# A decode block with cached attention: scalars as single elements, P turned on VectorE, and q with x stationary

## The chip, the cores and the metric

The kernel runs on one core of a Trainium2 chip (trn2). The time is device time in microseconds (us) of one execution. A run's time is about 1.8 us longer than the span of its profile (668.85 against 667.1, for example), and the two are never mixed here. Where several runs are told, the median is given with the lowest and the highest.

Words that return: PE is the matmul engine and PEld its weight loads, DVE is VectorE, ACT is ScalarE, POOL is GpSimd, SP is SyncE, whose queue issues nearly all loads here. The stream is the sequence of transfers on the core's 16 DMA engines. SBUF is the on-chip memory, PSUM the matmul's accumulators.

## The reference

Four tokens of width 640 go through a block with two branches that are summed: attention with 32 heads over a cache of 4,096 keys and values, and a gated feed-forward branch in which one scalar scale and one scalar shift stand.

```python
xn = layernorm(x)                                  # x: (4, 1, 640) bf16
q = (xn @ wq) as (B=4, H=32, 1, Dh=128)            # wq: (640, 4096)
p = softmax(q . k_cache * Dh**-0.5)                # k_cache: (4, 32, 4096, 128)
o = (p . v_cache) as (B, 1, H * Dh) @ wo           # v_cache like k_cache, wo: (4096, 640)
z1, z2 = halves of gelu(xn @ w_in)                 # w_in: (640, 1728)
g = w_sp * layernorm(z2) + b_sp                    # w_sp and b_sp: one number each
out = x + o + (z1 * g) @ w_out                     # w_out: (864, 640)
```

The two caches are 268 MB of the 282 MB that the kernel must read, and every byte of them is used once.

## The kernel before

Heads go in four groups of eight. Each group has four units of K and four of V (one for each token), 8.4 MB each. All of them pass through one large SBUF tile, `kv`, cut into slots; a load into a slot can start only when the last reader of the slot's old contents is done. The parts that the change touches:

```python
# two scalars, each broadcast to 128 partitions, on POOL's software queue
sb_bf = const.tile([P, 2], BF16)
nc.gpsimd.dma_start(out=sb_bf[:, 0:1], in_=B_w_sp.rearrange("a b -> (a b)").to_broadcast((P, 1)))
nc.gpsimd.dma_start(out=sb_bf[:, 1:2], in_=B_b_sp.to_broadcast((P, 1)))
...
# q: wq stationary, 160 matmuls with four columns each
for h in range(H):
    for c in range(DC):
        nc.tensor.matmul(q_ps[:, h, :], lhsT=wq[:, c, h * Dh:(h + 1) * Dh], rhs=xnT[:, c, :], ...)
...
# softmax of one group: exp four times over, PE transposes, copies, first fill of Zb
for half in range(2):
    x = ps_t.tile([P, 16, P], BF16, tag="x", name="x")
    for q in (2 * half, 2 * half + 1):
        p_q = ppool.tile([P, 8, HP, NE, M], BF16, tag="p", name="p")
        for e in range(NE):
            nc.scalar.activation(out=p_q[:, :, :, e, :], in_=S_ps[...].to_broadcast((P, 8, HP, M)), func=ACT.Exp, ...)
        for t in range(8):
            nc.tensor.transpose(x[:, 8 * (q % 2) + t, :], p_q[:, t].rearrange("p r e m -> p (r e m)"), IdP[:])
    for hp in range(HP):
        nc.vector.tensor_copy(out=xd[r0:r0 + 32, :, 16 * half:16 * half + 16], in_=x[r0:r0 + 32, :, r0:r0 + 32]...)
    z_fill(g, 0, (slice(16 * half, 16 * half + 16),))
z_fill(g, 1)
```

`Zb` holds the probabilities in the form in which 64 matmuls (called the O matmuls below) take them as weights against one unit of V. The first V load after a softmax overwrites a slot that these O matmuls still read, so the chain from scores to O matmuls decides when that load is issued.

## Time and profile before

| | before |
|---|---|
| time, median of 3 runs | 668.84 us (668.02 to 668.85) |
| profiled span | 665.9 us |
| bytes read from memory | 282.25 MB |
| mean rate over the span | 424 GB/s |
| busiest engine | DVE, 54% |
| TensorE | 46% |

A busy share says how much of the span an engine worked. The row that matters here is DMA in the 40 slices, shown in the prediction: it stands at 9 from the second slice to the last but one, so the kernel is bound by its stream. The groups of instructions that the change replaces are small beside that. From the page's groups (line, engine, operation, output from input, count, then busy us and mean ns, then idle time before):

```profile
L414 DVE COPY xd<-x 32x512 bf16<-32x512 bf16 x32 | 22.0, 687 | 20.7 <-PE x L410 20.0
L410 PE MATMUL x<-IdP,p 128*128 128x128 bf16 x128 | 16.5, 309 | 25.2 <-ACT p L406 12.9
...
L258 PE MATMUL misc<-xnT,kv 128*128 128x4 bf16 x160 | 4.4, 166 | 7.8 <-DMA kv<-in_A_wq_dram 7.8
```

The last row is q: PE waits 7.8 us for wq and is then busy for 4.4. The two rows above it are the turning of P, together with the copies behind it. They are there four times, once for each group of heads.

### The profile page before, as it was taken

To read this page: it belongs to the slowest core of one execution; us is meant where nothing else is said; L and a number is where in the kernel's file an instruction comes from. 1 tells how busy PE (TensorE), PEld (TensorE's weight loads), DVE (VectorE), ACT (ScalarE), POOL (GpSimd) and SP (SyncE) were. 2 spreads that over 40 slices of the span, in tenths; PEclk is the share of its full clock that TensorE was granted. 3 is DMA by queue.
4 is the path that set the end of the run, shared out by engine and by line. 5 is a ranking of instruction groups with operands and counts; after the bars stand their busy time and mean duration, and the time that the engine had idled before them with its cause. 6 is when DMAs were issued, how large, how long until landed. Compare 5 with 4: busy or idle time off the path is not lost.

```text
span 665.9 us, 6036 instructions
## 1 busy us (share of the span) xinstructions
PE 306.5 (46%) x2585; PEld 126.8 (19%) x2585; DVE 358.0 (54%) x318; ACT 93.3 (14%) x233; POOL 8.0 (1%) x27
## 2 busy tenths in 40 slices
PE   0656656526063546535425065551605336543355
PEld 0512211302011122211102022230201112122122
DVE  5179998446190749428356186743709165852002
ACT  1200000730200000450200000082020000046200
POOL 1000000000000000000000000000000000000000
PEclk9996787569578596676959587765867868677776
DMA  8999999999999999999999999999999999999996
GB/s 327 434 422 433 436 425 448 437 427 437 426 437 438 437 403 449 429 438 441 426 429 438 425 420 428 449 426 438 433 442 441 426 433 408 439 434 434 434 408 243
DMA packets 7874, 282.64 MB, mean 424 GB/s; under 512 B 948, under 2 KB 1320, under 8 KB 2088
## 3 DMA queue, kind: packets, MB, share of 16 engines
q1 hardware_dynamic: 7768, 282.25, 98.5%
q8 instruction: 20, 0.33, 0.2%
q14 instruction: 6, 0.05, 0.0%
q10 hardware_dynamic: 16, 0.01, 0.0%
q0 software_dynamic: 64, 0.00, 0.0%
HBM read 282.25 MB, written 0.01 MB: 424 GB/s over the span
## 4 chain that ended last, share of the span: by engine, by line
DMA 76%; DVE 10%; issue 10%; PE 2%; ACT 1%; DVEq 0%; SPq 0%; ACTq 0%
DMA kv<-in_A_k_cache_dram 66%; DVE kT L348 9%; DMA kv<-in_A_v_cache_dram 4%; DMA kv<-in_A_wo_dram 3%; DMA kv<-in_A_wq_dram 3%; PE misc L258 1%; ACT Zb L392 1%; ACT p L406 1%; DVE xd L414 1%; PE O L437 0%; PE proj L475 0%; PE x L410 0%; DVE om L457 0%; DVE m L366 0%; PE S L359 0%
## 5 line engine op out<-in xcount | busy, mean ns | idle before, releaser
L348 DVE STREAM_TRANSPOSE kT<-kv 128x2048 f32<-128x2048 f32 x128 | 283.4, 2277 | 134.2 <-DMA kv<-in_A_k_cache_dram 134.2
L359 PE MATMUL S<-kT,QZ 128*32 128x512 bf16 x1024 | 189.9, 505 | 237.5 <-DVE kT L348 237.5
L359 PEld LDWEIGHTS <-QZ 128*32 128x32 bf16 x1024 | 60.8, 112 | 359.9 <-issue 340.3
L437 PE MATMUL O<-kv,Zb 128*32 128x512 bf16 x1024 | 70.8, 431 | 34.4 <-DMA kv<-in_A_v_cache_dram 23.9
L392 ACT ACTIVATE Zb<-xd,MkE 32x256 bf16<-32x256 bf16 (+1 forms) x160 | 65.3, 454 | 108.3 <-PE O L437 99.1
L406 ACT ACTIVATE p<-S,negmax 128x512 bf16<-128x512 f32 x32 | 21.6, 694 | 398.2 <-DVE negmax L380 398.2
L444 DVE TENSOR_SCALAR R<-O,Mk 128x128 f32<-128x128 f32 x16 | 5.6, 351 | 106.2 <-PE O L437 106.2
L437 PEld LDWEIGHTS <-Zb 128*32 128x32 bf16 x1024 | 34.1, 106 | 69.2 <-issue 44.2
L414 DVE COPY xd<-x 32x512 bf16<-32x512 bf16 x32 | 22.0, 687 | 20.7 <-PE x L410 20.0
L410 PE MATMUL x<-IdP,p 128*128 128x128 bf16 x128 | 16.5, 309 | 25.2 <-ACT p L406 12.9
L410 PEld LDWEIGHTS <-p 128*128 128x128 bf16 x128 | 12.3, 140 | 30.2 <-ACT p L406 16.9
L454 PE MATMUL misc<-R,SelR 128*32 128x128 f32 x32 | 6.7, 293 | 24.0 <-DVE R L446 24.0
L446 DVE SCALAR_TENSOR_TENSOR R<-O,Mk,R 128x128 f32<-128x128 f32 x48 | 16.8, 351 | 1.7
L335 POOL COPY QZ<-q 32x32 bf16<-32x32 bf16 x16 | 5.1, 319 | 412.1 <-PE S L359 400.9
L475 PE MATMUL proj<-kv,oT 128*4 128x320 bf16 x64 | 8.4, 426 | 1.2 <-DMA kv<-in_A_wo_dram 1.0
L454 PEld LDWEIGHTS misc<-R,SelR 128*32 128x32 f32 x32 | 2.4, 112 | 31.4 <-DVE R L446 31.1
L366 DVE TENSOR_REDUCE m<-S 128x2 f32<-128x1024 f32 x4 | 4.9, 1225 | 6.0 <-PE S L359 6.0
L258 PE MATMUL misc<-xnT,kv 128*128 128x4 bf16 x160 | 4.4, 166 | 7.8 <-DMA kv<-in_A_wq_dram 7.8
L406 ACT ACTIVATION_READ_ACCUMULATOR p<-S,negmax 128x1 f32 x32 | 6.8, 212 | 0.0
L371 PE MATMUL misc<-dg,ones_f 128*128 128x256 f32 x8 | 3.0, 466 | 7.5 <-DVE dg L368 7.5
L457 DVE SCALAR_TENSOR_TENSOR om<-misc,rinv,MkH 32x1024 bf16<-32x1024 f32 x4 | 5.1, 1272 | 2.6 <-PE misc L454 2.6
L261 DVE CAST q_bf<-misc 128x128 bf16<-128x128 f32 x1 | 0.3, 292 | 11.3 <-PE misc L258 11.3
(92 smaller groups left out, 62.2 us busy)
## 6 DMA issues: line engine op xcount, KB each, us to landing
kv<-in_A_k_cache_dram SPq DMA_DIRECT2D x14, 4096.0 KB, 33.0
kv<-in_A_wq_dram SPq DMA_DIRECT2D x1, 5120.0 KB
kv<-in_A_v_cache_dram SPq DMA_DIRECT2D x1, 4096.0 KB, 38.4
kv<-in_A_wo_dram SPq DMA_DIRECT2D x2, 1280.0 KB, 28.7
kv<-in_B_w_in_dram SPq DMA_DIRECT2D x1, 2160.0 KB, 22.0
kv<-in_A_v_cache_dram SPq DMA_DIRECT2D x1, 2048.0 KB, 32.0
kv<-in_A_wo_dram SPq DMA_DIRECT2D x3, 640.0 KB, 20.7
kv<-in_A_v_cache_dram SPq DMA_DIRECT2D x1, 1536.0 KB
```

The source lines that it names most:

```text
L258: nc.tensor.matmul(q_ps[:, h, :], lhsT=wq[:, c, h * Dh:(h + 1) * Dh], rhs=xnT[:, c, :], start=(c == 0), stop=(c == DC - 1))
L348: nc.vector.transpose(kT[:].rearrange("p (t r) -> p t r", r=32), kw)
L359: nc.tensor.matmul(S_ps[32 * q:32 * q + 32, e], lhsT=QZ[:, b, 2 * kh + w, e, w0:w0 + 32], rhs=kb[:, i, :, e, :, w], start=(b == 0 and k < ...
L392: nc.scalar.activation(out=dst, in_=src, func=ACT.Copy, scale=MkE[r0:r0 + 32, e:e + 1])
L406: nc.scalar.activation(out=p_q[:, :, :, e, :], in_=S_ps[:, e, 8 * q:8 * q + 8, None, :].to_broadcast((P, 8, HP, M)), func=ACT.Exp, bias=ne ...
L410: nc.tensor.transpose(x[:, 8 * (q % 2) + t, :], p_q[:, t].rearrange("p r e m -> p (r e m)"), IdP[:])
L414: nc.vector.tensor_copy(out=xd[r0:r0 + 32, :, 16 * half:16 * half + 16], in_=x[r0:r0 + 32, :, r0:r0 + 32].rearrange("p t r -> p r t"))
L437: nc.tensor.matmul(O_ps[32 * q:32 * q + 32, :, :], lhsT=Zb[b % 2][:, w].rearrange("p h c -> p (h c)"), rhs=vv[:, w * 4 * Dh:(w + 1) * 4 * ...
L444: nc.vector.tensor_scalar(out=R, in0=O_ps[:, 0, :], scalar1=Mk4[:, 0:1], scalar2=None, op0=ALU.mult)
L446: nc.vector.scalar_tensor_tensor(out=R, in0=O_ps[:, c, :], scalar=Mk4[:, c:c + 1], in1=R, op0=ALU.mult, op1=ALU.add)
L454: nc.tensor.matmul(oh[:], lhsT=SelR[:, b].rearrange("p h b -> p (h b)"), rhs=state["R"][:, b, :], start=(b == 0), stop=(b == B - 1))
L475: nc.tensor.matmul(proj[32 * hf:32 * hf + B, 0:NO2], lhsT=oT[:, c, :], rhs=wo_t[g][:, c, hf * NO2:(hf + 1) * NO2], start=False, stop=(g == ...
```

## The change

Three things are done at once. The scalars are loaded as two single elements and spread to 128 partitions by a matmul with a row of ones. P is turned by one vector transpose of 32x32 blocks, followed by copies from quadrant to quadrant, half on DVE and half on ACT; exp is then computed once instead of four times. And q is computed with x as the weights and wq moving, which needs 40 matmuls for 160, and copies after them.

```diff
-    sb_bf = const.tile([P, 2], BF16)
-    nc.gpsimd.dma_start(out=sb_bf[:, 0:1], in_=B_w_sp.rearrange("a b -> (a b)").to_broadcast((P, 1)))
-    nc.gpsimd.dma_start(out=sb_bf[:, 1:2], in_=B_b_sp.to_broadcast((P, 1)))
+    sb_bf = const.tile([1, 2], BF16)                      # behind w_out on the SP queue
+    nc.sync.dma_start(out=sb_bf[:, 0:1], in_=B_w_sp)
+    nc.sync.dma_start(out=sb_bf[:, 1:2], in_=B_b_sp[None, :])
     ... cut ...
+            for j in range(NG):
+                nc.tensor.matmul(q4_ps[32 * j:32 * j + 32, hf * 512:hf * 512 + 512], lhsT=xnT[:, c, :],
+                                 rhs=wq[:, c, n0:n0 + 512], start=(c == 0), stop=(c == DC - 1))
     ... cut: eight copies of q4, half on DVE and half on ACT, then 32 small matmuls that select q3 ...
-    nc.gpsimd.tensor_copy(out=sb_f[:], in_=sb_bf[:])
+    nc.tensor.matmul(sb_ps[:], lhsT=one_bf[:], rhs=sb_bf[:], start=True, stop=True)
+    nc.vector.tensor_copy(out=sb_f[:], in_=sb_ps[:])
     ... cut: in softmax, the loops shown above are replaced by ...
+        for e in range(NE):
+            nc.scalar.activation(out=p_bf[:, :, e, :], in_=S_ps[:, e], func=ACT.Exp, ..., accum_out=rowsum[:, e:e + 1])
+        nc.vector.transpose(pT[:].rearrange("p t h x -> p (t h x)"), p_bf[:].rearrange("p t e m -> p (t e m)"))
+        for hp in range(HP):
+            for q in range(4):
+                op = nc.vector.tensor_copy if q < 2 else nc.scalar.copy
+                op(out=xd[32 * hp:32 * hp + 32, :, q, :], in_=pT[32 * q:32 * q + 32, :, hp, :].rearrange("p t x -> p x t"))
+        z_fill(g, 0)
         z_fill(g, 1)
```

More of the change, by code (lines that the diff above doesn't have):

```diff
@@ L68 @@
     ppool = ctx.enter_context(tc.tile_pool(name="ppool", bufs=3))
-    ps_t = ctx.enter_context(tc.tile_pool(name="ps_t", bufs=1, space=bass.MemoryType.PSUM))
     ps_s = ctx.enter_context(tc.tile_pool(name="ps_s", bufs=1, space=bass.MemoryType.PSUM))
     ps_o = ctx.enter_context(tc.tile_pool(name="ps_o", bufs=2, space=bass.MemoryType.PSUM))
-    ps_m = ctx.enter_context(tc.tile_pool(name="ps_m", bufs=1, space=bass.MemoryType.PSUM))
+    ps_m = ctx.enter_context(tc.tile_pool(name="ps_m", bufs=2, space=bass.MemoryType.PSUM))
     ps_j = ctx.enter_context(tc.tile_pool(name="ps_j", bufs=1, space=bass.MemoryType.PSUM))
@@ L102 @@
     nc.vector.memset(x_res[:], 0.0)
-    sb_bf = const.tile([P, 2], BF16)
-    nc.gpsimd.dma_start(out=sb_bf[:, 0:1], in_=B_w_sp.rearrange("a b -> (a b)").to_broadcast((P, 1)))
-    nc.gpsimd.dma_start(out=sb_bf[:, 1:2], in_=B_b_sp.to_broadcast((P, 1)))
-    sb_f = const.tile([P, 2], F32)
     n_in = DC * F2
@@ L191 @@
         nc.tensor.transpose(xT_ps[:, c, :], xn_v[:, c, :], ident_bf[:B, :B])
-    xnT = const.tile([P, DC, B], BF16)
-    nc.vector.tensor_copy(out=xnT[:], in_=xT_ps[:])
+    xnT = const.tile([P, DC, 32], BF16)
+    nc.vector.memset(xnT[:], 0.0)
+    nc.vector.tensor_copy(out=xnT[:, :, 0:B], in_=xT_ps[:])
     QL = 40
@@ L224 @@
     nc.vector.tensor_reduce(out=MkE[:], in_=I32[:].rearrange("p (e m) -> p e m", e=NE), axis=AX.X, op=ALU.add)
-    IdP = const.tile([P, P], BF16)
-    nc.vector.tensor_copy(out=IdP[:].rearrange("p (x q) -> p q x", q=4), in_=ident_bf[:].rearrange("p (q x) -> p q x", q=4))
     IdF = const.tile([P, P], F32)
@@ L232 @@
     nc.vector.tensor_reduce(out=MkH[:], in_=ident_f[:G, :G].rearrange("p (h b) -> p h b", b=B), axis=AX.X, op=ALU.add)
-    nc.vector.tensor_scalar(out=MkH[:], in0=MkH[:], scalar1=float(HP), scalar2=None, op0=ALU.mult)
     B32f = const.tile([G, B], F32)
@@ L237 @@
     nc.vector.tensor_copy(out=B32[:], in_=B32f[:])
-    Pm = const.tile([P, 4, HP, 32], BF16)
-    for hp in range(HP):
-        nc.vector.tensor_copy(out=Pm[:, :, hp, :].rearrange("p (a w) j -> p a w j", w=2),
-                              in_=ident_bf[:].rearrange("p (a j w) -> p a w j", a=2, w=2))
     NW = T // 4
@@ L252 @@
     proj = ps_j.tile([64, 512], F32)
-    q_ps = misc_ps([P, H, B], F32)
-    for h in range(H):
+    q4_ps = ps_s.tile([P, HG * Dh], F32, tag="S", name="q4")
+    for hf in range(2):
         for c in range(DC):
-            nc.tensor.matmul(q_ps[:, h, :], lhsT=wq[:, c, h * Dh:(h + 1) * Dh], rhs=xnT[:, c, :],
-                             start=(c == 0), stop=(c == DC - 1))
-    q_bf = const.tile([P, H * B], BF16)
-    nc.vector.tensor_copy(out=q_bf[:], in_=q_ps[:].rearrange("p h b -> p (h b)"))
-    q3_ps = misc_ps([P, 4, H * B], F32)
-    for kw in range(4):
-        nc.tensor.matmul(q3_ps[:, kw, :], lhsT=Pm[:, kw, :, :].rearrange("p a j -> p (a j)"), rhs=q_bf[:],
-                         start=True, stop=True)
-    q3 = const.tile([P, 4, H * B], BF16)
+            for j in range(NG):
+                n0 = j * HG * Dh + hf * 512
+                nc.tensor.matmul(q4_ps[32 * j:32 * j + 32, hf * 512:hf * 512 + 512], lhsT=xnT[:, c, :],
+                                 rhs=wq[:, c, n0:n0 + 512], start=(c == 0), stop=(c == DC - 1))
+    q4 = at_slot(0, HG * Dh * HP, n_q + 8 * D).rearrange("p (h k r j) -> p h k r j", h=HG, k=4, r=HP)
+    q4_in = q4_ps[:].rearrange("p (h a j w) -> p h a w j", h=HG, a=2, w=2)
+    for r in range(HP):
+        op = nc.vector.tensor_copy if r < 2 else nc.scalar.copy
+        for a in range(2):
+            op(out=q4[:, :, 2 * a:2 * a + 2, r, :], in_=q4_in[:, :, a])
+    SelJ = const.tile([P, NG, B], BF16)
+    nc.vector.tensor_copy(out=SelJ[:], in_=ident_bf[:].rearrange("p (j r) -> p j r", j=NG)[:, :, 0:B])
+    q3_ps = misc_ps([P, 4, HG, NG * B], F32)
+    for h in range(HG):
+        for kw in range(4):
+            nc.tensor.matmul(q3_ps[:, kw, h, :], lhsT=q4[:, h, kw].rearrange("p r j -> p (r j)"),
+                             rhs=SelJ[:].rearrange("p j b -> p (j b)"), start=True, stop=True)
+    q3 = const.tile([P, 4, HG, NG * B], BF16)
     nc.vector.tensor_copy(out=q3[:], in_=q3_ps[:])
@@ L280 @@
                 nc.tensor.matmul(zT_ps[:n, part, fc, :], lhsT=w,
-                                 rhs=xnT[:, c, :], start=(c == 0), stop=(c == DC - 1))
+                                 rhs=xnT[:, c, 0:B], start=(c == 0), stop=(c == DC - 1))
     zT = const.tile([P, 2, FC, B], F32)
@@ L287 @@
     nc.scalar.activation(out=zT[:FL, :, FC - 1, :], in_=zT_ps[:FL, :, FC - 1, :], func=ACT.Gelu_apprx_tanh)
-    nc.gpsimd.tensor_copy(out=sb_f[:], in_=sb_bf[:])
+    one_bf = const.tile([1, P], BF16)
+    nc.vector.memset(one_bf[:], 1.0)
+    sb_ps = misc_ps([P, 2], F32)
+    nc.tensor.matmul(sb_ps[:], lhsT=one_bf[:], rhs=sb_bf[:], start=True, stop=True)
+    sb_f = const.tile([P, 2], F32)
+    nc.vector.tensor_copy(out=sb_f[:], in_=sb_ps[:])
     z1 = zT[:, 0, :, :]
@@ L333, in fill_qz @@
             r0 = 32 * hp
-            c0 = (g * HG + NE * hp) * B
             nc.gpsimd.tensor_copy(out=QZ[r0:r0 + 32, :, :, :, 8 + 8 * hp],
-                                  in_=q3[r0:r0 + 32, :, c0:c0 + NE * B].rearrange("p a (e b) -> p b a e", b=B))
+                                  in_=q3[r0:r0 + 32, :, NE * hp:NE * hp + NE, g * B:g * B + B].rearrange("p a e b -> p b a e"))
     state = {}
@@ L381, in softmax_max, with z_fill @@
         return negmax
-    def z_fill(g, b, halves=(slice(0, TC),)):
+    def z_fill(g, b):
         xd = state[("xd", g)]
-        for hs in halves:
-            n0, n1 = hs.start // 4, hs.stop // 4
-            for hp in range(HP):
-                r0 = 32 * hp
-                src = xd[r0:r0 + 32, 8 * b:8 * b + 8, hs].rearrange("p x (y c) -> p x y c", c=4)
-                for e in range(NE):
-                    dst = Zb[b % 2][r0:r0 + 32, :, NE * hp + e, :].rearrange("p (x y) c -> p x y c", x=8)[:, :, n0:n1, :]
-                    nc.scalar.activation(out=dst, in_=src, func=ACT.Copy, scale=MkE[r0:r0 + 32, e:e + 1])
+        for hp in range(HP):
+            r0 = 32 * hp
+            src = xd[r0:r0 + 32, C2 * b:C2 * b + C2].rearrange("p x q (y c) -> p (x q y) c", c=4)
+            for e in range(NE):
+                nc.scalar.activation(out=Zb[b % 2][r0:r0 + 32, :, NE * hp + e, :], in_=src, func=ACT.Copy,
+                                     scale=MkE[r0:r0 + 32, e:e + 1])
     def softmax(g):
@@ L396, in softmax @@
         S_ps = state.pop(("S", g))
-        xd = small.tile([P, 32, TC], BF16, tag="xd", name="xd", bufs=1)
-        state[("xd", g)] = xd
-        rs = small.tile([P, NE, 4], F32, tag="rs")
-        for half in range(2):
-            x = ps_t.tile([P, 16, P], BF16, tag="x", name="x")
-            for q in (2 * half, 2 * half + 1):
-                p_q = ppool.tile([P, 8, HP, NE, M], BF16, tag="p", name="p")
-                for e in range(NE):
-                    nc.scalar.activation(out=p_q[:, :, :, e, :],
-                                         in_=S_ps[:, e, 8 * q:8 * q + 8, None, :].to_broadcast((P, 8, HP, M)),
-                                         func=ACT.Exp, bias=negmax[:, e:e + 1], scale=scale, accum_out=rs[:, e, q:q + 1])
-                for t in range(8):
-                    nc.tensor.transpose(x[:, 8 * (q % 2) + t, :], p_q[:, t].rearrange("p r e m -> p (r e m)"), IdP[:])
-            for hp in range(HP):
-                r0 = 32 * hp
-                nc.vector.tensor_copy(out=xd[r0:r0 + 32, :, 16 * half:16 * half + 16],
-                                      in_=x[r0:r0 + 32, :, r0:r0 + 32].rearrange("p t r -> p r t"))
-            z_fill(g, 0, (slice(16 * half, 16 * half + 16),))
+        p_bf = ppool.tile([P, TC, NE, M], BF16, tag="p", name="p")
+        rowsum = small.tile([P, NE], F32, tag="rowsum")
+        for e in range(NE):
+            nc.scalar.activation(out=p_bf[:, :, e, :], in_=S_ps[:, e], func=ACT.Exp, bias=negmax[:, e:e + 1], scale=scale,
+                                 accum_out=rowsum[:, e:e + 1])
+        pT = ppool.tile([P, TC, HP, B * C2], BF16, tag="p", name="pT")
+        nc.vector.transpose(pT[:].rearrange("p t h x -> p (t h x)"), p_bf[:].rearrange("p t e m -> p (t e m)"))
+        xd = small.tile([P, B * C2, 4, TC], BF16, tag="xd", name="xd", bufs=1)
+        state[("xd", g)] = xd
+        for hp in range(HP):
+            for q in range(4):
+                op = nc.vector.tensor_copy if q < 2 else nc.scalar.copy
+                op(out=xd[32 * hp:32 * hp + 32, :, q, :], in_=pT[32 * q:32 * q + 32, :, hp, :].rearrange("p t x -> p x t"))
+        z_fill(g, 0)
         z_fill(g, 1)
-        rowsum = small.tile([P, NE], F32, tag="rowsum")
-        nc.vector.tensor_reduce(out=rowsum[:], in_=rs[:], axis=AX.X, op=ALU.add)
         cs = misc_ps([G, 1], F32)
@@ L431, in emit_V @@
         vv = unit(("v", v))
-        order = list(range(NW))
-        if b == 0:
-            order.sort(key=lambda w: w % 8 // 4)
-        for n, w in enumerate(order):
-            q = n % 4
+        for w in range(NW):
+            q = w % 4
             nc.tensor.matmul(O_ps[32 * q:32 * q + 32, :, :], lhsT=Zb[b % 2][:, w].rearrange("p h c -> p (h c)"),
-                             rhs=vv[:, w * 4 * Dh:(w + 1) * 4 * Dh], start=(n < 4), stop=(n >= NW - 4))
+                             rhs=vv[:, w * 4 * Dh:(w + 1) * 4 * Dh], start=(w < 4), stop=(w >= NW - 4))
         if b == 0:
```

## The prediction

> **What bounds the kernel now.** I read the page's 40 slices first, then the chain that ended last, the stretches of the first and last microseconds, and the DMA queue's own timeline. The slices:
>
> ```profile
> DVE  5179998446190749428356186743709165852002
> ...
> DMA  8999999999999999999999999999999999999996
> GB/s 327 434 422 433 436 425 448 437 427 437 426 437 438 437 403 449 429 438 441 426 429 438 425 420 428 449 426 438 433 442 441 426 433 408 439 434 434 434 408 243
> ```
>
> From the second slice to the last but one the DMA row never leaves 9, while every engine has idle slices. The page reads 282.25 MB from HBM; the stretch from 8.75 to 650 us shows a DMA share of 1.00 at 432 GB/s. So 282.25 / 0.432 = 653 us of the 665.9 us are transfer, and only three things can move the end: bytes (the change leaves them alone, apart from a few hundred), holes in the stream, and what runs before its start and after its end. The chain agrees:
>
> ```profile
> DMA 76%; DVE 10%; issue 10%; PE 2%; ACT 1%; DVEq 0%; SPq 0%; ACTq 0%
> ```
>
> A warning on that row: its DVE pieces (10%) are a transpose of K that frees a slot, followed by a transfer that lands 30 us later. Between the two the transfer mostly stands in the queue behind others, so these pieces are no cost either. What matters is how long a transfer queues. The K loads take 33.0 us from issue to landing and the V loads 34.9, while an 8.4 MB unit by itself takes 8.39 / 0.432 = 19.4 us: some 14 us of slack. The tightest case is the V load issued at 607.04 us, which lands at 636.14: 29.1 - 19.4 = 9.7 us.
>
> The stream has one visible hole. Stretches of the first microseconds (columns: stretch, length, busy time of five engines, clock, DMA share, GB/s; a packet counts where it starts, so a share may exceed 1):
>
> ```profile
> 4.00:5.00 1.00, 0.00 (x0) 0.00 (x0) 1.00 (x2) 0.00 (x0) 0.00 (x0) 1.00 1.15 492
> 5.00:6.00 1.00, 0.00 (x0) 0.00 (x0) 0.98 (x5) 0.00 (x0) 0.00 (x0) 1.00 0.11 41
> 6.00:7.00 1.00, 0.00 (x0) 0.00 (x0) 0.95 (x2) 0.00 (x0) 0.00 (x0) 1.00 0.21 82
> 7.00:8.00 1.00, 0.00 (x0) 0.00 (x0) 0.99 (x4) 0.29 (x1) 0.00 (x0) 1.00 1.27 533
> ```
>
> The wq rows are packets of 40 KB that take about 1.5 us each. Fifteen of the 16 engines start their second packet at 4.3 to 4.8 us and would be free again at 5.9 to 6.3; yet nearly all start the third only at 6.9 to 8.1. In the packet records of this trace each of these late starts comes 12 ns after a 16-byte packet of the software queue, which carries nothing but the two broadcast scalars:
>
> ```profile
> q0 software_dynamic: 64, 0.00, 0.0%
> ```
>
> Means: free at 6.0, next start at 7.75, so about 1.75 us lost per engine. Later packets of 40 KB follow each other without a gap.
>
> **What the Trainium skill says.** "DMA: Bandwidth & Descriptors", section "Queues, rings and completion order": each DMA engine goes round-robin between the queue rows that have work, a packet at a time. The trace agrees as far as it shows 16-byte packets between the 40 KB ones; that an engine stands still until the software queue's packet can run is my reading, not the page's. Same page, "Why a DMA increments its semaphore by 16 and not by 1": a one-element transfer on the hardware queue uses one engine alone. No run shows it yet; it means that the new scalar loads can delay one engine only, by a packet or two. "VectorE: DVE Perf Modes", "The three transpose paths": the vector transpose turns 32x32 blocks and cannot span banks, hence the copies between quadrants. Its 2,048-element fp32 transpose takes 2,277 ns here, 1.11 ns per column element; I take the same for 1,024 elements of bf16.
>
> **The change part by part.**
>
> *Scalars.* Two software-queue broadcasts (128 elements each) go; two one-element loads join the SP queue behind w_out, and a 1x128 matmul spreads them. They should land with w_out at some 24 us; they are needed at about 31 us, where the scale and shift now stands. Effect on the stream: the hole closes, -1.75 us; against it some 0.1 us on one engine. Since the last bytes come from the slowest of 16 engines I count -1.6.
>
> *q with x stationary.* Before: 160 weight loads and matmuls, 18.09 to 22.54 = 4.45 us, then 0.30 (copy), 0.6 (4 matmuls), 0.7 (copy): q3 at 24.2. After: 40 matmuls of 512 columns over four column groups. The O matmuls are of this form: 64 in 3.64 us, 0.057 each; so 40 x 0.057 + 0.3 = 2.6 us. Then four copies of 128x512 from PSUM on DVE (0.69 us, like the q cast) beside four on ACT (0.69, like exp): 2.8. Then 32 matmuls with full weight loads at 0.05 = 1.6, and the cast 0.7. Sum 7.7 against 6.1: q3 some 1.6 us later, or level with before if wq lands 1.7 us earlier. K1's first half, which needs wq's slot, was issued at 22.9 us and is only due to run when wq, w_in, w_out and K0 (16.9 MB) are through, about 43 us; its second half, which now also waits for q4 in that slot, is due ten us later. The first K transpose waits for its DMA until 36.2 us; the vector work before it ended at 31.6. All of this is hidden.
>
> *Softmax.* Its last instance, in order of the chain:
>
> ```profile
> 591.63 2.80 ACT p L406 x8
> ...
> 594.47 1.05 PE x L410 x8
> ...
> 595.61 0.68 DVE xd L414
> ...
> 598.49 0.68 ACT Zb L392 x2
> ...
> 604.35 0.69 ACT Zb L392 x2
> ...
> 605.08 1.94 PE O L437 x32
> 607.04 29.11 DMA kv<-in_A_v_cache_dram
> ```
>
> Before: from 591.54 (negmax) to 607.04, 15.5 us, with eight exps, 32 PE transposes, eight copies of 0.69 us and, on ACT, sixteen fills of 0.34 us on the way to the first V unit. After: two exps (2 x 0.90 with their accumulator reads = 1.8), one transpose of 1,024 elements (1.15), then eight copies of 32x256 on each of DVE and ACT (ACT at 0.41 between starts, as a fill of that size: 3.3; DVE less), eight fills of 0.46 (3.7), then 64 matmuls (3.6). Sum 13.5: the V load is issued about 2 us sooner. The slack it had was 9.7 us, so its landing does not move. Per group DVE saves about 2 us and PE 4 us, and ACT loses six exps but gains eight copies; none of them is on the path.
>
> *Tail.* The instructions after the last V piece are the same ones in the same order (I compared the PE streams: only semaphore numbers differ, and one wait goes). From 655.9 us the old tail took 10 us, and the new one should too.
>
> *Instruction fetches.* PE's program shrinks from 5,081 rows to 4,643. Before, 20 fetches of 16 KB ran on the same DMA engines, one holding an engine for about 1 us, and they are part of why the engines finish spread out:
>
> ```profile
> 657.00:658.00 1.00, 0.50 (x6) 0.24 (x7) 0.93 (x3) 0.00 (x0) 0.00 (x0) 0.50 0.76 303
> 658.00:659.00 1.00, 1.00 (x8) 0.60 (x5) 0.10 (x1) 0.00 (x0) 0.00 (x0) 0.50 0.55 221
> 659.00:660.00 1.00, 1.00 (x9) 0.35 (x7) 0.81 (x1) 0.00 (x0) 0.00 (x0) 0.50 0.52 202
> 660.00:661.00 1.00, 0.74 (x10) 0.48 (x8) 0.46 (x1) 0.00 (x0) 0.00 (x0) 0.55 0.31 119
> ```
>
> One or two fetches fewer are worth 0 to 1 us, depending on whether the slowest engine is spared; I count -0.2.
>
> Sum: 668.84 - 1.6 - 0.2 = 667.0 us.
>
> **Rivals.** (1) The hole belongs to the start of the hardware queue (its first descriptors), and the software packets merely wait beside it. For it: other things start then too, and the second software transfer, near 10.5 us, opens no hole. Against it: sixteen late starts, each right behind a software packet. Then the time stays at 668.5 to 669. (2) A wait takes the place of the one removed: the longer q chain or the copies on ACT hold back K's slots or the first V unit. For it: ACT does fill, copy and exp in one line. Against it: 20 us of slack at the start and 9.7 at the end. Copies of twice the estimated time would still be hidden; a gap of 5 us would need an error of 15, and would give 674. (3) The compute saved shortens the run as such, 2 us in each of four softmaxes: 660. The full DMA row speaks against it. (4) The engines' spread shifts with the fetches and the slowest gets one more: up to +1 us on either outcome.
>
> **Range and chances.** I give the closed hole two chances in three (666 to 668), the unchanged one a little under one in three (668 to 669.5). The spread of the engines adds a microsecond either way, so 664.8 to 669.3. Two per cent is 13 us: more than all time outside the stream, so faster is next to impossible, and slower needs a stall that the slack speaks against.
>
> **What would show it.** Right: the software queue gone from the list of queues; a DMA share near 1 in the stretch from 5 to 8 us; wq's first reader on PE at about 16.4 us instead of 18.09; the middle at 432 GB/s; the last V load still landing one unit's time after the one before it. Wrong: an empty stretch at 5 to 7 us as before (step 1); a hole in the DMA row near 115 to 140 us or 590 to 610 us, or the first K transpose waiting for PE or ACT instead of its DMA (the slack); a tail longer than 10 us from the last V matmul.

## The result, and the profile after

| | before | after |
|---|---|---|
| time, median of 6 runs | 668.88 us (668.02 to 669.06) | 666.77 us (665.57 to 666.91) |
| profiled span | 665.9 us | 665.0 us |
| instructions | 6,036 | 5,565 |
| q's first matmul on PE starts at | 18.09 us | 16.16 us |
| last V unit multiplied: first DVE step on it starts at | 656.59 us | 654.73 us |

The ratio is 0.9965, with a 95% interval of 0.9952 to 0.9978. Ratios here are the mean time of one kernel's fast runs over that of the other's of the same rounds, so they are not quite the ratio of the medians quoted. The change takes 2.1 us off, 0.3%.

The runs of both kernels fall in two clusters about 1 us apart: before mostly near 668.9 and some near 668.0, after near 666.8 and 665.6. The two profiles fell in different ones (the profiled run of before took 667.67 us, below all six timed ones, that of after 666.74), so their spans (665.9 and 665.0) understate the gain. The tail below shows it. The last row of the table is free of that, since it comes before the tail's last matmuls, and it moved by 1.86 us.

From the page of the kernel after, the rows of DMA and of the rate, its queues and its chain:

```profile
DMA  9999999999999999999999999999999999999995
GB/s 372 424 440 425 426 441 444 438 431 439 434 418 439 434 413 455 434 427 438 419 434 439 434 418 421 452 442 434 427 426 431 438 439 412 464 418 423 429 415 219
...
q1 hardware_dynamic: 7772, 282.25, 98.6%
q8 instruction: 18, 0.29, 0.2%
...
DMA 74%; DVE 10%; issue 10%; PE 3%; ACT 2%; DVEq 0%; SPq 0%; ACTq 0%
```

The first slice rose from 327 to 372 GB/s and the software queue is gone from the list. The rest of the row is as full as it was. The first microseconds of the kernel after (columns: stretch, length, busy time with count of PE, PEld, DVE, ACT and POOL, clock, DMA share, GB/s):

```profile
5.00:6.00 1.00, 0.00 (x0) 0.00 (x0) 1.00 (x5) 0.00 (x0) 0.00 (x0) 1.00 1.51 655
6.00:7.00 1.00, 0.00 (x0) 0.00 (x0) 0.97 (x4) 0.00 (x0) 0.00 (x0) 1.00 0.19 82
7.00:8.00 1.00, 0.00 (x0) 0.00 (x0) 0.99 (x3) 0.21 (x1) 0.00 (x0) 1.00 1.32 573
```

The 0.19 in the middle is no hole. A packet counts where it starts, and the packets are 40 KB each; over the three microseconds the mean is 437 GB/s, where before it was 219 (41, 82 and 533).

The new groups, from the page's groups:

```profile
L417 ACT COPY xd<-pT 32x256 bf16<-32x256 bf16 x32 | 19.6, 613 | 5.7 <-DVE pT L410 5.2
...
L417 DVE COPY xd<-pT 32x256 bf16<-32x256 bf16 x32 | 11.7, 364 | 0.6
...
L410 DVE STREAM_TRANSPOSE pT<-p 128x1024 bf16<-128x1024 bf16 x4 | 5.0, 1245 | 6.3 <-ACT p L406 6.3
```

And the last softmax on the timeline (start, duration, instructions, idle time before and what ended it):

```profile
592.01 5.02 ACT L417 COPY xd<-pT 32x256 bf16<-32x256 bf16 x8 [1.31 <-DVE pT L410]
...
597.06 7.39 ACT L397 ACTIVATE Zb<-xd,MkE 32x256 bf16<-32x256 bf16 x16
600.79 6.08 PE L434 MATMUL O<-kv,Zb 128*32 128x512 bf16 x64 [9.78 <-ACT Zb L397]
606.92 10.87 SPq L148 DMA_DIRECT2D kv<-in_A_v_cache_dram  x5
```

Negmax was ready at 589.16, so this chain took 17.8 us to the issue of the V load; before it took 15.5. The end of the tail, first on the timeline of before and then on that of after:

```profile
661.45 1.25 PE L475 MATMUL proj<-kv,oT 128*4 128x320 bf16 x16 [0.28 <-DVE oT L468]
```

```profile
659.58 2.30 PE L472 MATMUL proj<-kv,oT 128*4 128x320 bf16 x16 [0.28 <-DVE oT L465]
```

The same sixteen matmuls start 1.87 us sooner and take 1.05 us longer, at a granted clock of 0.50 in this profile and 1.00 in that of before. That is the difference between the spans' 0.9 us and the 1.9 us of the table.

### The profile page after: what moved, and what is told of

It is laid out like the page before. It is cut to its first block, busy times and chain, and to the rows that moved or that the text cites. A ratio compares the mean times of both kernels' runs of the same rounds, so it can differ in the third digit from the quotient of the medians.

```text
span 665.0 us, 5565 instructions
## 1 busy us (share of the span) xinstructions
PE 294.0 (44%) x2366; PEld 111.6 (17%) x2366; DVE 353.5 (53%) x319; ACT 91.3 (14%) x189; POOL 6.2 (1%) x24
## 3 DMA queue, kind: packets, MB, share of 16 engines
q1 hardware_dynamic: 7772, 282.25, 98.6%
## 4 chain that ended last, share of the span: by engine, by line
DMA 74%; DVE 10%; issue 10%; PE 3%; ACT 2%; DVEq 0%; SPq 0%; ACTq 0%
DMA kv<-in_A_k_cache_dram 65%; DVE kT L356 9%; DMA kv<-in_A_v_cache_dram 4%; DMA kv<-in_A_wo_dram 3%; DMA kv<-in_A_wq_dram 2%; PE O L434 1%; PE q L252 1%; ACT xd L417 1%; PE proj L472 1%; ACT Zb L397 0%; DVE kv L260 0%; PE S L367 0%; ACT kv L260 0%; ACT p L406 0%; DVE om L454 0%
## 5 line engine op out<-in xcount | busy, mean ns | idle before, releaser
L367 PE MATMUL S<-kT,QZ 128*32 128x512 bf16 x1024 | 185.7, 495 | 232.2 <-DVE kT L356 232.2
L434 PE MATMUL O<-kv,Zb 128*32 128x512 bf16 x1024 | 75.2, 457 | 66.2 <-ACT Zb L397 39.1
L397 ACT ACTIVATE Zb<-xd,MkE 32x256 bf16<-32x256 bf16 x128 | 57.7, 497 | 106.5 <-PE O L434 105.1
L406 ACT ACTIVATE p<-S,negmax 128x512 bf16<-128x512 f32 x8 | 5.4, 683 | 395.1 <-DVE negmax L388 395.1
L417 ACT COPY xd<-pT 32x256 bf16<-32x256 bf16 x32 | 19.6, 613 | 5.7 <-DVE pT L410 5.2
L417 DVE COPY xd<-pT 32x256 bf16<-32x256 bf16 x32 | 11.7, 364 | 0.6
L410 DVE STREAM_TRANSPOSE pT<-p 128x1024 bf16<-128x1024 bf16 x4 | 5.0, 1245 | 6.3 <-ACT p L406 6.3
L260 DVE CAST kv<-q 128x512 bf16<-128x512 f32 x4 | 2.5, 682 | 9.4 <-PE q L252 9.4
L252 PE MATMUL q<-kv,xnT 128*32 128x512 bf16 x40 | 4.5, 629 | 5.1 <-DMA kv<-in_A_wq_dram 5.1
L422 PE MATMUL misc<-rowsum,SelPe 128*32 128x1 f32 x16 | 2.1, 200 | 9.0 <-ACT p L406 9.0
```

The source lines that it names most:

```text
L252: nc.tensor.matmul(q4_ps[32 * j:32 * j + 32, hf * 512:hf * 512 + 512], lhsT=xnT[:, c, :], rhs=wq[:, c, n0:n0 + 512], start=(c == 0), stop= ...
L367: nc.tensor.matmul(S_ps[32 * q:32 * q + 32, e], lhsT=QZ[:, b, 2 * kh + w, e, w0:w0 + 32], rhs=kb[:, i, :, e, :, w], start=(b == 0 and k < ...
L397: nc.scalar.activation(out=Zb[b % 2][r0:r0 + 32, :, NE * hp + e, :], in_=src, func=ACT.Copy, scale=MkE[r0:r0 + 32, e:e + 1])
L406: nc.scalar.activation(out=p_bf[:, :, e, :], in_=S_ps[:, e], func=ACT.Exp, bias=negmax[:, e:e + 1], scale=scale, accum_out=rowsum[:, e:e + 1])
L417: op(out=xd[32 * hp:32 * hp + 32, :, q, :], in_=pT[32 * q:32 * q + 32, :, hp, :].rearrange("p t x -> p x t"))
L434: nc.tensor.matmul(O_ps[32 * q:32 * q + 32, :, :], lhsT=Zb[b % 2][:, w].rearrange("p h c -> p (h c)"), rhs=vv[:, w * 4 * Dh:(w + 1) * 4 * ...
```

## The experiments

**How to read them.** Since the clock of the tail blurs a single span, and the medians mix the two clusters, I read each run at three places: its median, the start of the DVE step that follows the last V unit (called R), and the mean rate over a fixed stretch in which its hole lies. In the runs on scalars R measures what the stream lost before it. Both R and the rate come from one profile of each kernel, and a profiled run can lie apart from the others of its kernel (before's was 0.35 us below its fastest timed run, e6's 0.5 above its next slowest), so differences of half a microsecond in them are not read as effects. All runs gave correct results.

| run | scalars | median (lowest to highest) | ratio to before | R |
|---|---|---|---|---|
| before | two broadcasts, software queue, at the start | 668.88 (668.02 to 669.06) | 1 | 656.59 |
| after | single elements, SP queue | 666.77 (665.57 to 666.91) | 0.9965 | 654.73 |
| e1_scalars_only | before + single elements, SP queue | 666.90 (666.23 to 666.95) | 0.9971 | 654.68 |
| e2_no_scalars | after + the old broadcasts | 668.98 (668.01 to 669.03) | 1.0002 | 656.90 |
| e3_hw_broadcast | before + two broadcasts on the SP queue | 668.14 (668.10 to 668.82) | 0.9995 | 656.13 |
| e4_late_sw | before + software broadcasts later | 668.93 (668.57 to 669.12) | 1.0002 | 656.49 |
| e5_sw_single | before + single elements, software queue | 667.18 (666.26 to 667.24) | 0.9968 | 655.01 |
| e6_distinct | e1 + two loads of 128 elements, rows apart | 666.00 (665.94 to 667.40) | 0.9960 | 655.46 |
| e7_double | e3 with four broadcasts | 670.15 (669.54 to 671.37) | 1.0017 | 659.26 |
| e12_adjacent | e1 + two loads of 128 adjacent elements | 667.88 (667.02 to 668.28) | 0.9983 | 656.39 |

### Which part of the change

The theory: the gain is the scalars alone, and the other two parts are hidden behind the stream. The rival: the shorter compute is worth something too.

**e1_scalars_only**: the kernel before with the scalars' part of the change and nothing else.

```diff
-    nc.gpsimd.dma_start(out=sb_bf[:, 0:1], in_=B_w_sp...to_broadcast((P, 1)))   # and one for b_sp
+    nc.sync.dma_start(out=sb_bf[:, 0:1], in_=B_w_sp)                            # and one for b_sp
-    nc.gpsimd.tensor_copy(out=sb_f[:], in_=sb_bf[:])
+    nc.tensor.matmul(sb_ps[:], lhsT=one_bf[:], rhs=sb_bf[:], start=True, stop=True)
+    nc.vector.tensor_copy(out=sb_f[:], in_=sb_ps[:])
```

> The kernel before with the scalar part of the change alone. Theory (the software-queue broadcasts hold every DMA engine at the start; nothing else of the change counts): the whole gain, 666.6 to 667.0 us against 668.9 (-2.0), the first q matmul at 16.2 us instead of 18.09, a DMA share near 1.5 in the stretch from 5 to 6 us. Rival A (the shorter PE program, two instruction fetches fewer, makes the gain): 668.9, since PE's program is not shorter here. Rival B (the compute saved in q and softmax makes it): 668.9.

It measured 666.90 us, ratio 0.9971 (0.9959 to 0.9984), and R at 654.68 against 654.73 of the full change. This is the whole gain. It has 20 instruction fetches, as before, so the two that the full change saves are not needed for it.

**e2_no_scalars**: the full change, with the old broadcasts put back.

```diff
-    nc.sync.dma_start(out=sb_bf[:, 0:1], in_=B_w_sp)                            # and one for b_sp
+    nc.gpsimd.dma_start(out=sb_bf[:, 0:1], in_=B_w_sp...to_broadcast((P, 1)))   # and one for b_sp
```

> The changed kernel with the two software-queue broadcasts put back. Theory: no gain, 668.5 to 669.1 us, hole from 5 to 7 us back, first q matmul at 18.1 us. Rival A: it keeps up to 1 us of gain (667.9). Rival B: it keeps the gain (666.8).

It measured 668.98 us, ratio 1.0002 (0.9989 to 1.0014). Its first microseconds:

```profile
5.00:6.00 1.00, 0.00 (x0) 0.00 (x0) 1.00 (x5) 0.00 (x0) 0.00 (x0) 1.00 0.09 41
6.00:7.00 1.00, 0.00 (x0) 0.00 (x0) 0.93 (x3) 0.00 (x0) 0.00 (x0) 1.00 0.32 123
```

The hole is back and with it the time. q, softmax and the 18 fetches together are worth nothing that these rounds can tell from zero.

### What makes the hole

The prediction put it down to the software queue: an engine stands still until that queue's packet can run. Rivals: the broadcast itself does it, on any queue; or it is the start of the stream, beside which the packets merely wait.

**e4_late_sw**: the kernel before, with the same two software broadcasts held back until the layernorm's result; they are issued at 11.92 and 12.59 us.

```diff
+    nc.gpsimd.tensor_copy(out=sb_bf[:], in_=xnT[:, 0, 0:2])    # makes the loads wait
     nc.gpsimd.dma_start(out=sb_bf[:, 0:1], in_=B_w_sp...to_broadcast((P, 1)))
```

> The kernel before with the software-queue broadcasts issued only after the normalised x exists, at about 10.5 us. If the first software packet on an engine always holds it: the hole moves to about 13 to 17 us and the time stays at 668.5 to 669.1. If the hole needs the coincidence with the start of the stream: first q matmul at 16.2 us, no hole later, 666.6 to 667.2 us.

The time stayed (668.93 us), but the hole left its place. Over 5 to 8 us the rate is now 437 GB/s, as in the kernel after, and it stands here instead, with the same mean of 219 GB/s over 15 to 18 us:

```profile
15.00:16.00 1.00, 0.00 (x0) 0.00 (x0) 0.00 (x0) 0.00 (x0) 0.00 (x0) 1.00 0.85 328
16.00:17.00 1.00, 0.77 (x29) 0.77 (x29) 0.00 (x0) 0.00 (x0) 0.00 (x0) 1.00 0.13 35
```

The hole travels with the loads of the scalars. The rival of the stream's start is out.

**e3_hw_broadcast**: the same two broadcasts, on the SP queue behind w_out, and nothing on the software queue.

```diff
-    nc.gpsimd.dma_start(out=sb_bf[:, 0:1], in_=B_w_sp...to_broadcast((P, 1)))
+    nc.sync.dma_start(out=sb_bf[:, 0:1], in_=B_w_sp...to_broadcast((P, 1)))     # behind w_out; b_sp likewise
```

> The kernel before with the same two 128-element broadcasts issued from the SP queue behind w_out. If the software queue is what holds the engines: the gain is kept, 666.6 to 667.2 us, first q matmul at 16.2 us. If it is the 256 two-byte elements, whatever queue carries them: no gain, or the hole moves to where they run, behind w_out, 668.5 to 669.

There is no hole at the start, and q begins at 16.00 us; but a hole opens where these loads stand in the queue:

```profile
22.00:23.00 1.00, 0.81 (x18) 0.81 (x18) 0.14 (x1) 0.00 (x0) 0.72 (x3) 1.00 0.78 232
23.00:24.00 1.00, 1.00 (x23) 1.00 (x21) 0.00 (x0) 0.00 (x0) 0.60 (x2) 1.00 0.28 96
```

The time is 668.14 us, ratio 0.9995 (0.9981 to 1.0009). The software queue is not needed for the loss.

**e5_sw_single**: the reverse, the kernel before with single elements on the software queue at the start.

```diff
-    nc.gpsimd.dma_start(out=sb_bf[:, 0:1], in_=B_w_sp...to_broadcast((P, 1)))
+    nc.gpsimd.dma_start(out=sb_bf[:, 0:1], in_=B_w_sp)          # tile [1, 2]; b_sp likewise; matmul as in e1
```

> The kernel before with the scalars as single elements (and the spreading matmul), but still issued on the software queue at the start. If the count of two-byte elements makes the hole: nearly the whole gain, 666.7 to 667.3 us, first q matmul at 16.2 us. If the mere use of the software queue at the start makes it: 668.5 to 669 us, first q matmul near 18 us.

667.18 us, ratio 0.9968 (0.9954 to 0.9982), and 437 GB/s over 5 to 8 us, although the queue still has its 64 packets. So the use of the queue does not make the hole; what costs is the broadcast, on either queue. One observation stays unexplained: on the software queue the whole hole comes with the first broadcast. The packets of the second, near 10.5 us in before, open none: over 8 to 11 us that kernel moves 437 GB/s, as the kernel after does.

**e7_double**: e3 with four broadcasts in place of two.

```diff
+    nc.sync.dma_start(out=dummy[:, 0:1], in_=B_b_sp.to_broadcast((P, 1)))       # and the same into dummy[:, 1:2]
```

> The kernel of the third run (both broadcasts on the SP queue behind w_out) with two more unused broadcasts right behind them, four in all. If each broadcast costs its elements: the hole doubles and the time grows by another 1.2 us, to 669.2 to 669.7. If the hole is paid once for the kind of transfer: 668.1 to 668.4.

670.15 us, and R 3.1 us later than in e3. The hole is now five microseconds long:

```profile
22.00:23.00 1.00, 0.88 (x20) 0.88 (x20) 0.07 (x1) 0.00 (x0) 0.79 (x3) 1.00 0.63 184
23.00:24.00 1.00, 1.00 (x22) 1.00 (x21) 0.00 (x0) 0.00 (x0) 0.55 (x2) 1.00 0.10 23
24.00:25.00 1.00, 1.00 (x25) 1.00 (x24) 0.00 (x0) 0.00 (x0) 0.00 (x0) 1.00 0.20 66
25.00:26.00 1.00, 0.82 (x14) 0.73 (x13) 0.00 (x0) 0.14 (x2) 0.18 (x1) 1.00 0.34 131
26.00:27.00 1.00, 0.42 (x2) 0.45 (x2) 0.27 (x2) 0.98 (x3) 0.00 (x0) 1.00 0.42 164
```

### What it is about a broadcast

A broadcast to 128 partitions is 128 elements of two bytes, all from one address. Is it the small elements, or the address?

**e6_distinct**: e1, and two more loads of 128 elements that nobody uses, from rows 1,280 bytes apart.

```diff
+    nc.sync.dma_start(out=dummy[:, 0:1], in_=B_w_out[0:P, 0:1])
+    nc.sync.dma_start(out=dummy[:, 1:2], in_=B_w_out[P:2 * P, 0:1])
```

> The kernel with the scalar part alone, plus two unused loads of 128 two-byte elements from 256 different HBM addresses, on the SP queue behind w_out, where the broadcasts of the third run stood. If small elements as such hold the engines: about 668.1 us as there, with a hole near 22 to 24 us. If it is that all 128 reads of a broadcast go to one address: 666.7 to 667.2 us and no hole of that size.

**e12_adjacent**: the same with the 128 elements side by side, 256 bytes in all.

```diff
-    nc.sync.dma_start(out=dummy[:, 0:1], in_=B_w_out[0:P, 0:1])
+    nc.sync.dma_start(out=dummy[:, 0:1], in_=B_w_out[0:1, 0:P].rearrange("a n -> n a"))   # and row 1 likewise
```

> As the run with distinct rows (the scalars as single elements, and two unused loads of 128 two-byte elements on the SP queue behind them), except that each unused load now takes its 128 elements from adjacent addresses, 256 bytes in a row, instead of from 128 rows 1,280 bytes apart. Theory A, the engines are held because all reads of a broadcast go to one and the same address: no hole at 22 to 25 us, median 666.0 to 667.0. Theory B, it is enough that the reads fall into one small region of memory: a hole of some 2 us at 22 to 25 us as with the two broadcasts on the SP queue, median 668.1 to 669. A hole of about half the size with 667 to 668 would mean that both count.

e6 measured 666.00 us and e12 667.88. I had first read e6 to mean that only reads of one and the same address hold the engines. e12 does not bear that out: its addresses all differ, and it has a hole.

```profile
22.00:23.00 1.00, 0.98 (x22) 0.98 (x22) 0.00 (x0) 0.00 (x0) 0.85 (x3) 1.00 0.62 194
23.00:24.00 1.00, 1.00 (x22) 1.00 (x21) 0.00 (x0) 0.00 (x0) 0.48 (x2) 1.00 0.48 162
```

The mean rate from 20 to 30 us sizes them all on one scale. e1 has 445 GB/s there. A run with the rate r lost 10 us times (445 - r) / 445:

| run | extra loads behind w_out | GB/s over 20 to 30 us | lost, us | R later than e1, us |
|---|---|---|---|---|
| e1_scalars_only | none | 445 | 0 | 0 |
| e6_distinct | 2 x 128 elements, 1,280 bytes apart | 415 | 0.7 | 0.8 |
| e3_hw_broadcast | 2 x 128 elements, one address | 374 | 1.6 | 1.5 |
| e12_adjacent | 2 x 128 elements, adjacent | 370 | 1.7 | 1.7 |
| e7_double | 4 x 128 elements, one address | 274 | 3.8 | 4.6 |

(In e3 and e7 these loads stand in place of e1's single elements, in e6 and e12 beside them.) The size depends on the stretch that is taken: over 18 to 32 us the five rates are 422, 422, 387, 386 and 311 GB/s, which gives 0, 0, 1.2, 1.2 and 3.7 us. So 256 elements of two bytes cost 1.2 to 1.7 us when their addresses are close together, whether equal or adjacent, and between nothing and 0.7 us when they are far apart. That e6 lost anything is not shown: its profiled run, at 667.40 us, was the slowest of its five, and cluster by cluster its times (666.90 and 667.40; 665.94 to 666.00) lie about e1's (666.71 to 666.95; 666.23). Theory A of e12, one and the same address, falls, since e12 has a hole. Theory B, one small stretch of memory, fits the stream, where e12 loses as much as e3. The median does not settle it: 667.88 us lies in the band, 667 to 668, that the expectation had given to both counting, so whether equal addresses add something is open. e1 and e3 ran on one chip, e5, e6 and e7 on a second, e12 on a third, which the last column does not correct for; e5, with single elements, has R at 655.01. What in the memory or the engines makes close addresses slow is not shown by any of these runs.

### How much slack the softmax had

Theory: the copies on ACT are off the path, with microseconds to spare. Rival: the slack is so small that a little more puts a hole behind each softmax.

**e8_act_once**: the kernel after with all sixteen copies of a softmax on ACT, none on DVE. **e9_act_twice**: the same, and each copy made twice.

```diff
-            for q in range(4):
-                op = nc.vector.tensor_copy if q < 2 else nc.scalar.copy
+            for q in range(4):               # e9: for q in [0, 1, 2, 3] * 2
+                op = nc.scalar.copy
```

> The changed kernel with all sixteen copies between quadrants of each softmax on ACT (none on DVE): the softmax chain grows by 8 x 0.63 = 5.0 us. In the changed kernel's trace the last such V load is issued at 606.9 us and its data starts to move at about 634.5 - 19.4 = 615.1. Theory (the softmax hides behind the queue): no change, 666.7 to 667.1 us. If the softmax were on the path: 671 us for the last group alone.

> As the run before, but every one of the sixteen copies is made twice: the softmax chain grows by 24 x 0.63 = 15.1 us. That is more than the 8.2 us of slack of the last group and about the 15 us of the others. Theory: a hole of some 7 to 9 us near 616 to 624 us and up to 1 us in each of the three others: 674 to 678 us. If something else than the queue absorbs it: less than 670.

Both are misses. e8 took 668.64 us (667.72 to 669.99, 4 runs; ratio to before 1.0001, 0.9987 to 1.0014), 1.9 us more than the kernel after; e9 took 706.21 us (703.49 to 708.62; ratio 1.056, 1.0534 to 1.0586), 39 us more. Stretches of e8 around its last softmax, and of e9 around its first:

```profile
610.00:615.00 5.00, 3.62 (x44) 1.26 (x36) 1.22 (x4) 2.46 (x6) 0.00 (x0) 0.75 0.98 368
615.00:620.00 5.00, 4.19 (x68) 2.05 (x68) 0.81 (x3) 2.97 (x8) 0.00 (x0) 1.00 0.58 236
```

```profile
136.00:140.00 4.00, 0.00 (x0) 0.00 (x0) 0.00 (x0) 3.85 (x7) 0.00 (x0) 0.50 0.65 281
140.00:150.00 10.00, 5.56 (x56) 2.13 (x60) 0.00 (x0) 7.88 (x18) 0.00 (x0) 0.50 0.01 2
150.00:152.00 2.00, 0.85 (x16) 0.23 (x8) 1.02 (x3) 1.01 (x3) 0.00 (x0) 0.98 0.93 295
```

In e9 the stream stands still for ten microseconds while ACT copies and fills and DVE has nothing to do: the next V load waits for the O matmuls, they wait for the fills, and the queue behind is empty. Against 432 GB/s the three stretches lack 1.4 + 10.0 + 0.6 = 12.0 us. The V load was issued at 150.90 us, where the kernel after issues it at 133.49: 17.4 us later for a hole of 12.0, so the slack was 5.4 us. The loads themselves say the same. From its issue to the first O matmul that reads it, this load took 21.95 us in e9, where it had no queue before it, and 27.25 us in the kernel after: 5.3 us of queueing. In e8 it was issued 5.9 us later than in the kernel after, took 22.2 us, and the stream lost about 1.9 us (279 and 421 GB/s in the two five-microsecond stretches from 135 us), which leaves 4.0. So the slack behind the first softmax of the kernel after is 4 to 5.4 us. At the last one e8 issues its V load 6.75 us later than the kernel after (613.67 against 606.92) and first reads it 3.26 us later (637.78 against 634.52), which leaves 3.5. Both expectations had rested on more, because I had taken 19.4 us, a unit at full rate, for an unqueued load, which takes 22. In e9 the loss is taken four times: the stream also stands from 310 to 319, from 478 to 486 and from 645 to 653 us. In e8 it shows behind the first and the last softmax, 3.2 us in the span of its profile, which was of the slowest of its four runs.

### Versions for the tail

What is left outside the stream is the tail. **e10_tail4** is the kernel after with the output projection spread over four column groups instead of two; the halves are added at the end.

```diff
-                nc.tensor.matmul(proj[32 * hf:32 * hf + B, 0:NO2], lhsT=oT[:, c, :], ...)
+                r = 64 * (c % 2) + 32 * hf
+                nc.tensor.matmul(proj[r:r + B, 0:NO2], lhsT=oT[:, c, :], ...)
-    nc.vector.tensor_copy(out=o_bf[:], in_=proj[:, 0:NO2])
+    nc.scalar.copy(out=o_hi[:], in_=proj[64:128, 0:NO2])
+    nc.vector.tensor_tensor(out=o_bf[:], in0=proj[0:64, 0:NO2], in1=o_hi[:], op=ALU.add)
```

> The changed kernel with the output projection spread over four column groups of the PE array instead of two, and an ACT copy plus a DVE add at the end. A candidate to beat both. Theory: with the transfers over, the tail is bound by PE at half the granted clock (16 matmuls in 2.30 us); they should take 1.2 us, the selection matmuls should start 0.4 us sooner, and the copy adds 0.45: 665.5 to 666.2 us against 666.8. If the tail is bound by the last landing of wo instead: 666.8 or, with the copy, 667.2.

666.20 us (666.09 to 666.33), ratio 0.9957 (0.9944 to 0.9969): 0.6 us below the median of after, and the two clusters are gone. The sixteen last matmuls took 1.55 us, between the 1.25 and 2.30 seen above. It beats before. Against after nothing is shown: the two intervals overlap, and two runs of after (665.57 and 665.68) were faster than any of e10.

**e11_tail5** is e10 with the masking of `om` split, five heads on DVE and three on ACT.

```diff
-        nc.vector.scalar_tensor_tensor(out=om[:], ...)                       # all eight heads
+        nc.vector.tensor_tensor(out=om[:, 0:5, :], in0=oh[...], in1=mkr[...], op=ALU.mult)
+        for h in range(5, HG):
+            nc.scalar.activation(out=om[:, h, :], in_=oh[:], func=ACT.Copy, scale=mkr[:, h:h + 1])
```

> The four-column-group version with the masking of the attention output in the tail shared between DVE (five heads) and ACT (three heads, with the mask and the reciprocal multiplied ahead). Theory: the tail is a chain of single instructions, and this one shrinks from 1.27 to about 0.9 us: 665.8 to 666.0 us against 666.2. If the last landing of wo bounds the tail: no change.

666.25 us (666.19 to 666.36), ratio 0.9963 (0.9950 to 0.9977): no gain over e10. Its timeline tells why:

```profile
657.07 0.81 DVE L459 TENSOR_TENSOR om<-misc,mkr 32x640 bf16<-32x640 f32 x1 [0.73 <-PE misc L454]
...
657.91 0.86 ACT L462 ACTIVATE om<-misc,mkr 32x128 bf16<-32x128 f32 x3 [33.87 <-DVE om L459]
```

ACT's three heads do not run beside DVE's five but after them. The two end at 658.77, 1.70 us after the start, where the one DVE instruction took 1.27.

## Why the prediction was right or wrong

The time (666.77 for 667.0) and the sense of it were right. The number did not hang on the step that failed: the 1.6 us was read from the gaps between the packets of before, and it comes out whatever makes these gaps, as long as single elements make none. The softmax was estimated 4.3 us too short; that this cost nothing is luck, since the slack was overestimated as well and turned out just large enough. By its own steps:

- **The kernel is bound by the stream, and compute saved is worth nothing: shown.** e2 has the shorter q and softmax code and runs at 1.0002 of before. Rival 3, the compute saved as a gain, is out.
- **The hole at 5 to 7 us closes: right, and its size as well.** Counted were 1.6 us. By the rates over 3 to 11 us (323 before, 404 after), 8 us times 81 / 404 is 1.6 us; R moved by 1.86 and the medians by 2.1. Rival 1, the start of the hardware queue, is out by e4. q's first matmul was due at about 16.4 us and came at 16.16.
- **That the software queue makes the hole: wrong.** The step that failed is the reading "that an engine stands still until the software queue's packet can run". The packets were the right ones, but what costs is the two broadcasts that they carry, not the queue: on the SP queue the same loads cost nearly as much (e3: R 1.5 us later than e1's, where before's is 1.9 later), and single elements on the software queue cost at most 0.3 us (e5: R 655.01 against 654.68). Had the change moved the broadcasts to the SP queue, this step would have foretold the full gain, where e3 has a ratio of 0.9995.
- **The single elements are nearly free: borne out.** e1 has two of them on the SP queue, e5 on the software queue, and neither shows a hole. With e1's loads the SP queue carries four packets more than before (7,772 for 7,768), which fits a load that uses one engine alone.
- **Fewer fetches, -0.2: no such term.** e1 has 20 fetches and the whole gain; e2 has 18 and none.
- **q at 7.7 us, hidden: hidden, but mis-sized.** The forty matmuls took 4.46 us where 2.6 were counted, and ACT's four copies began only after DVE's four (20.66 to 23.14, then 23.24 to 25.29) where "beside" was assumed. q3 was ready at 27.87 us, 11.7 after the first matmul. The first K transpose waits for its DMA as before, until 34.53 us.
- **Softmax at 13.5 us: wrong, 17.8, which is longer than the 15.5 of before.** The terms: ACT's copies 0.613 us each for the 0.41 taken from a fill (5.0 for 3.3 in all), and the 64 O matmuls 6.08 us for 3.6. The 0.41 was a misreading: it is the mean over sixteen fills of which eight are only 32x128, and the kernel after starts its 32x256 fills every 0.46 us. The clock granted from 600 to 607 us was 0.59, while of the O matmuls of before the last 32 ran at 1.00. So the change made this chain slower, and the V load was issued at 606.92 us with no gain against 607.04, although the stream was almost two microseconds ahead.
- **Slack of 9.7 us at the end and "some 14 us" elsewhere: both too large.** The conclusion stands, since e2 shows the longer chain still hidden, but two things in the term were wrong. An unqueued unit is read 22 us after its issue, not 19.4; and the median over all V loads hides the first one behind each softmax, which queues for 5.3 us only. "Copies of twice the estimated time would still be hidden" was close to the edge: in e8 ACT's copies took 10.0 us, three times the estimate of 3.3, and the run lost 1.9 us. Rival 2, a new wait, did not come true in the change, but it was nearer than the prediction had it, and dearer: priced once, at 674 us, it came behind all four softmaxes in e9, 39 us in all.
- **The tail of 10 us: the same instructions, but not always the same time.** From R to the end of the last DVE step it took 6.6 us in the profile of before and 7.7 in that of after, and the difference goes with the projection's clock (0.50 against 1.00). Rival 4 had put about 1 us of spread on the DMA engines; clusters 1 us apart are there, and the profiles suggest the clock of the tail as their cause: the last sixteen matmuls, where they run on two column groups, took 2.29 or 2.30 us in ten profiles and 1.25 in the other two, before and e7. e10, with four column groups, has no clusters. This is argued, not shown; the granted clock alone does not fix the time either, since at 0.50 the sixteen matmuls took 1.55 us in e10 and 1.24 in e11.

## What to carry to other kernels

A load of a few hundred bytes is not free because it is small: broadcasting two scalars from memory to 128 partitions cost this kernel's stream 1.2 to 1.9 us, on either queue (before, e3), so load one element and spread it with a matmul. In a kernel bound by its stream, ask for each saving whether it moves a transfer, and put back one part of a bundled change at a time to see which part counts. Slack is what a load queues beyond the time of an unqueued load of the same size, read at the one load that follows the suspected chain; a median over all loads hides it.

## What the Trainium skill lacked or had wrong

- "DMA: Bandwidth & Descriptors" does not tell what a load of 128 two-byte elements costs other transfers. In its "Rules for kernel authors" it says that a strided last dimension becomes one descriptor for each element; the runs show what that costs a full stream: 1.2 to 1.6 us for two broadcasts of one address (e3), 1.2 to 1.7 for two loads of adjacent elements (e12), 3.7 to 3.8 for four broadcasts (e7), and 0 to 0.7 for two loads of elements 1,280 bytes apart (e6).
- "VectorE: DVE Perf Modes", in its section on the TRN2 errata, gives ScalarE 224 cycles and one for each element between SBUF tiles. For 256 elements at its 1.2 GHz that is an estimate of 400 ns; the strided bf16 copy of 32x256 took 613 ns, and DVE's 364.
- "TensorE: Matmul & The Clock Gate", Part 1, tells that the clock is halved after idle time until some microseconds of work have passed. The trace agrees in the durations: the forty q matmuls took 0.111 us each at the start of PE's work, the O matmuls of the same form 0.057. The page warns that clock events in a trace have been seen to be unreliable; it does not say that the granted clock of a profile can miss the slow start, as it does here: it reads 1.00 from 16 to 21 us, while these q matmuls ran at half speed.
